# Attention and token/channel mixer on one core: strided loads ahead of the next x, the last group's u summed beforehand, a 128-row short chunk

## The chip, the cores and the metric

One core of a Trainium2 chip runs the kernel. The metric is device time of one execution in microseconds (us), lower is better, as the median of several timed runs. A profiled execution gives the trace that is read below; its span is the time from the first to the last instruction. The engines are TensorE (PE, with its weight loads PEld), VectorE (DVE), ScalarE (ACT), GpSimd (POOL) and SyncE (SP), which here issues every DMA.

## The reference

```
x  = concat over 8 heads of softmax(mask(q k^T / 8)) v      # 8 batches, 576 rows, 64 per head -> 512 columns
     heads 0-3: local mask (0 <= i-j < 32);  heads 4-7: strided mask (j <= i, i%32 == j%32)
h  = relu(x^T w_tok1) w_tok2                                # token mix: 576 -> 256 -> 576
u  = x + h^T
out = u + relu(u w_ch1) w_ch2                               # channel mix: 512 -> 1536 -> 512
```

All of it is float32. In the strided heads each of 32 residues is an 18 by 18 attention.

## The kernel before

Every matrix product is made of three products of rounded parts (high by high, high by low, low by high), accumulated in PSUM: `xh`/`xlo`, `uh`/`ul`, `gh`/`gl` and the weights `t1h`/`t1l` and so on are such pairs. ACT makes the high part, DVE (for some weights POOL) the low part by subtraction.

The 8 x 576 rows go through the channel mix in nine groups of 512 (`mlp(grp, ...)`). A group has twelve up projections (L524, 12 matmuls each) and twelve down projections (L538, 12 matmuls each, into four PSUM tiles `acc`). Up projection fc+2 is written ahead of down projection fc. After a group, each `acc` gets `uh` (L560, DVE) and `ul` (L562, POOL, in the last group DVE) added into one of two `ot` buffers and is sent out (L563).

Between these matmuls PE does the work of the coming batches. The local heads go over PE (L170, L197, L207, softmax on DVE and ACT). The strided heads of batches 0 and 1 go over PE as well; those of batches 2 to 7 are made by `strided` without PE: POOL multiplies (L342, 27 products into two `sprod` buffers), DVE reduces each product (L343), then a softmax (L346 to L352) and 27 more pairs (L359, L361). The results go to DRAM (`xs<-sb`, L363), and `load_x` brings a batch's `x` back in (L370, L372), in five row chunks. There is one `x` buffer. `tok1` (token mix 1, L384 xh on ACT, L387 xlo on DVE, L396 matmuls) takes the chunks in turn, two banks of PSUM held; `tok2` (token mix 2, L427 transposes of x and L433) makes `u`.

576 rows are four chunks of 128 and one of 64. The fifth chunk stands in x twice, in rows 0 to 63 and 64 to 127. Its two terms for each half of the outputs are `(t1h[:64], xlo[:64])`, a matmul over 64 rows, and `(t1l[:], xh)` over 128 rows, in which `t1l` holds the rounded weights above and their low part below.

Order: up to the end of group 0 the instructions follow a list of step names, `ORDER`, each name one step of a generator; `in_order` chains every instruction to the one before it on its engine. The names that matter here: `A`/`D` up and down projections of group 0, `V0` the first local unit of batch 2, `Y0` to `Y3` the last 64 rows of batch 0 through `tok2`, four column blocks, in the order Y3, Y0, Y2, Y1; `X1` the loads of batch 1's x, `B` its `tok1`, `C` its `tok2`, and `G` the call `strided` for batch 2. `G` alone is not chained; like all later work it is placed by a scheduler that works from a timeline of its own, with instructions of `strided` given a low priority. Also, `do_strided` holds its instructions back until the latest `x` load has been issued:

```
with tc.issue_after(state["loaded"].ins):
    strided(sp, b, 3000)
```

Once placed, each engine's order is fixed: an instruction that waits holds up everything behind it on its engine. SP is one such queue for all DMAs.

## Time and profile before

| | |
|---|---|
| timed runs | 888.44, 886.46, 879.77 us; median 886.46 |
| profiled execution | 882.51 us, of which the span is 880.5 us |
| mean granted TensorE clock | 0.982 |
| busy share of the span | PE 94%, DVE 55%, POOL 46%, ACT 24% |

The runs lie within 1% of each other. PE's busy time counts the matmuls as they overlap in the pipeline, so 94% does not say that 6% are left. The span has three parts: some 80 us at the start, in which weights are converted and batch 0 goes through attention and token mixes; the stretch to some 680 us, in which PE's projections go along with POOL's and DVE's strided heads; and a last stretch with PE alone.

### The profile page before, as it was taken

What the parts mean: (1) busy time and instruction counts of PE and PEld (TensorE: products, weight loads), DVE (VectorE), ACT (ScalarE), POOL (GpSimd) and SP (SyncE); (2) the same over time, 40 slices, a digit from 0 to 9 for tenths busy, and PEclk for the clock granted to TensorE, in tenths of its full rate; (3) what the DMA queues carried; (4) which work ended last, traced back from release to release, by engine and by line L of the source; (5) the groups of instructions that cost most, each with busy time, mean ns of one, the idle gap of its engine ahead of it and who ended that gap; (6) DMA issues with size and microseconds to landing.
All of it is one profiled execution on the core that took longest, in us unless ns stands there. A gap on an engine that the chain in (4) does not pass through costs nothing.

```text
span 880.5 us, 16250 instructions
## 1 busy us (share of the span) xinstructions
PE 826.7 (94%) x6820; PEld 659.7 (75%) x6820; DVE 487.8 (55%) x941; ACT 208.5 (24%) x378; POOL 404.0 (46%) x385
## 2 busy tenths in 40 slices
PE   4588999799978999999999999999999999999996
PEld 3366787578856787787887887778788877888885
DVE  4789873667567755775577567645774222112112
ACT  3676652221112212211212112112111121111110
POOL 0112300786577765795679477845885002002000
PEclk9979999999998999999999999999999999999998
DMA  7647754302542323023402421223112001001001
GB/s 256 198 157 251 240 191 123 130 1 92 132 160 63 102 54 123 28 80 88 157 28 79 142 97 40 74 64 115 35 53 77 11 1 48 1 1 41 8 1 48
DMA packets 57639, 78.99 MB, mean 90 GB/s; under 512 B 18144, under 2 KB 39776, under 8 KB 57568
## 3 DMA queue, kind: packets, MB, share of 16 engines
q1 hardware_dynamic: 57568, 77.97, 27.5%
q8 instruction: 53, 0.87, 0.4%
q14 instruction: 18, 0.15, 0.1%
HBM read 59.54 MB, written 18.28 MB: 88 GB/s over the span
## 4 chain that ended last, share of the span: by engine, by line
PE 65%; POOL 13%; DVE 9%; DMA 7%; issue 2%; SPq 2%; ACT 1%; DVEq 0%; POOLq 0%; ACTq 0%
PE h L524 25%; PE acc L538 23%; POOL sprod L342 9%; PE t L433 6%; POOL sprod L359 4%; PE t L396 4%; DMA sb<-in_ks 3%; PE t L427 3%; DVE ss L343 2%; DMA lk<-in_kT 1%; PE t L207 1%; DVE xlo L387 1%; PE t L170 1%; SPq L372 1%; DMA xs<-sb 1%
## 5 line engine op out<-in xcount | busy, mean ns | idle before, releaser
L342 POOL TENSOR_TENSOR sprod<-sb,sa 128x576 f32<-128x576 f32 (+6 forms) x162 | 175.1, 1110 | 133.8 <-DMA sb<-in_ks 114.8
L359 POOL TENSOR_TENSOR sprod<-sa,ss 128x448 f32<-128x448 f32 (+7 forms) x162 | 162.9, 1038 | 34.3 <-DVE ss L352 24.9
L524 PE MATMUL h<-ul,w1h 128*128 128x512 f32 x432 | 170.7, 395 | 0.0
L524 PE MATMUL h<-uh,w1l 128*128 128x512 f32 x432 | 169.5, 392 | 0.0
L538 PE MATMUL acc<-gh,w2l 128*128 128x512 f32 x432 | 169.3, 392 | 0.0
L524 PE MATMUL h<-uh,w1h 128*128 128x512 f32 x432 | 168.4, 396 | 0.9 <-DVE gl L530 0.9
L538 PE MATMUL acc<-gl,w2h 128*128 128x512 f32 x432 | 168.7, 390 | 0.0
L538 PE MATMUL acc<-gh,w2h 128*128 128x512 f32 x432 | 165.6, 394 | 0.2 <-ACT gh L528 0.2
L530 DVE SCALAR_TENSOR_TENSOR gl<-h,gh 128x512 fp32r<-128x512 f32 x108 | 74.0, 686 | 141.5 <-ACT gh L528 141.3
L528 ACT ACTIVATE gh<-h 128x512 fp32r<-128x512 f32 x108 | 64.4, 599 | 317.7 <-PE h L524 304.3
L343 DVE TENSOR_REDUCE ss<-sprod 128x9 f32<-128x576 f32 (+6 forms) x162 | 90.8, 570 | 55.4 <-POOL sprod L342 54.3
L361 DVE TENSOR_REDUCE sb<-sprod 128x64 f32<-128x64 f32 (+8 forms) x162 | 91.4, 571 | 36.9 <-POOL sprod L359 35.9
L562 POOL TENSOR_TENSOR ot<-ot,ul 128x512 f32<-128x512 f32 x32 | 41.2, 1295 | 136.5 <-DVE ot L560 136.4
L524 PEld LDWEIGHTS h<-uh,w1h 128*128 128x128 f32 x432 | 81.0, 188 | 18.4 <-DVE gl L530 1.4
L538 PEld LDWEIGHTS acc<-gh,w2h 128*128 128x128 f32 x432 | 81.2, 188 | 17.6 <-ACT gh L528 0.7
L524 PEld LDWEIGHTS h<-uh,w1l 128*128 128x128 f32 x432 | 81.6, 189 | 16.7
L524 PEld LDWEIGHTS h<-ul,w1h 128*128 128x128 f32 x432 | 81.4, 189 | 16.8
L538 PEld LDWEIGHTS acc<-gh,w2l 128*128 128x128 f32 x432 | 81.1, 188 | 17.1
L538 PEld LDWEIGHTS acc<-gl,w2h 128*128 128x128 f32 x432 | 81.1, 188 | 16.3
L387 DVE TENSOR_TENSOR xlo<-x,xh 128x512 fp32r<-128x512 f32 (+1 forms) x45 | 40.0, 905 | 33.8 <-ACT xh L384 33.7
L438 DVE TENSOR_TENSOR ul<-t,uh 128x512 fp32r<-128x512 f32 (+7 forms) x64 | 28.8, 454 | 42.6 <-ACT uh L436 42.4
L436 ACT CAST uh<-t 128x512 fp32r<-128x512 f32 (+7 forms) x64 | 25.5, 399 | 108.8 <-PE t L433 108.7
(97 smaller groups left out, 881.0 us busy)
## 6 DMA issues: line engine op xcount, KB each, us to landing
w_raw<-in_w SPq DMA_DIRECT2D x24, 512.0 KB
out_t<-ot SPq DMA_DIRECT2D x36, 256.0 KB
lv<-in_vw SPq DMA_DIRECT2D x8, 520.0 KB
x<-xs SPq DMA_DIRECT2D x8, 512.0 KB
lv<-in_vw SPq DMA_DIRECT2D x6, 650.0 KB
xl<-lx SPq DMA_DIRECT2D x14, 256.0 KB
x<-xl SPq DMA_DIRECT2D x7, 512.0 KB
sa<-in_qs SPq DMA_DIRECT2D x6, 576.0 KB
```

The lines of the kernel that those rows point to most:

```text
L342: nc.gpsimd.tensor_tensor(out=pr, in0=k_t[:, n0:n0 + n], in1=q_t[:, i:i + 1].to_broadcast([P, n, D]), op=ALU.mult)
L343: nc.vector.tensor_reduce(out=s_t[:, i, n0:n0 + n], in_=pr, axis=AX.X, op=ALU.add)
L359: nc.gpsimd.tensor_tensor(out=pr, in0=v_t[:, d0:d0 + nd, :n], in1=s_t[:, i:i + 1, :n].to_broadcast([P, nd, n]), op=ALU.mult)
L361: nc.vector.tensor_reduce(out=o_t[:, i, d0:d0 + nd], in_=pr, axis=AX.X, op=ALU.add)
L387: nc.vector.tensor_tensor(out=xlo, in0=x, in1=xh.bitcast(F32), op=ALU.subtract)
L396: nc.tensor.matmul(ph[m], l, r, start=(c == 0 and k == 0), stop=(short and k == 1), skip_group_check=True)
L433: nc.tensor.matmul(pu[:, :n], l[:, cs], r[:, m, t0:t1], start=False, stop=(m == 1 and k == 2), skip_group_check=True)
L524: nc.tensor.matmul(ph, l[:, cc, fs], r, start=(cc == 0 and k == 0), stop=(cc == NCC - 1 and k == 2))
L528: nc.scalar.activation(out=gh, in_=ph, func=AF.Relu)
L530: nc.vector.scalar_tensor_tensor(out=gl, in0=ph, scalar=0.0, in1=gh.bitcast(F32), op0=ALU.max, op1=ALU.subtract)
L538: nc.tensor.matmul(acc[cc], l[:, fc, cs], r, start=(fc == 0 and k == 0), stop=(fc == NFC - 1 and k == 2))
L562: add.tensor_tensor(out=o_t, in0=o_t, in1=ul.bitcast(F32), op=ALU.add)
```

## The change

Four edits. (1) `G` moves in ORDER from behind `D10 V0 V0` to behind `Y3`, ahead of `X1`; its first two instructions, the loads of q and k (`sa`, `sb`), are now chained in the order, and for batch 2 the hold behind the x load is dropped. (2) In the last group, `uh + ul` is summed into `whole`, a tile in the place of `x`, during the group, and the sum is added to `acc` in one instruction at the end; each column block keeps a buffer of its own. (3) The last group's last two down projections are written as one, column block by column block. (4) The lower half of `t1h`'s fifth chunk is set to zero on POOL, once, and the 64-row matmul of token mix 1 becomes one over 128 rows.

```diff
+            differ("t2").memset(t1h[64:, NSC - 1].bitcast(F32), 0.0)
...
-                    terms = ((t1h[:64, c, ms], xlo[:64]), (t1l[:, c, ms], xh))
+                    terms = ((t1h[:, c, ms], xlo), (t1l[:, c, ms], xh))
...
-    ORDER = """... O A11 V0 Y3 A11 A11 Y0 Y3 Y3 Y2 Y0 Y0 Y1 Y2 Y2 D9 Y1 X1 Y1 V0 D10 V0 V0 G D11 V0 B ..."""
+    ORDER = """... O A11 V0 Y3 G A11 A11 Y0 Y3 Y3 Y2 Y0 Y0 Y1 Y2 Y2 D9 Y1 X1 Y1 V0 D10 V0 V0 D11 V0 B ..."""
...
-            if n != "G":
-                for i in traced[begun:]:
+            got = traced[begun:] if n != "G" else traced[begun:begun + 2]
+            for i in got:
...
-        def down_proj(fc):
-            gh, gl = g.pop(fc)
+        def down_proj(*fcs):
+            gs = [g.pop(fc) for fc in fcs]
             for cc in range(NCC):
                 cs = slice(P * cc, P * cc + P)
-                for k, (l, r) in enumerate(((w2h, gh), (w2h, gl), (w2l, gh))):
-                    nc.tensor.matmul(acc[cc], l[:, fc, cs], r, start=(fc == 0 and k == 0), stop=(fc == NFC - 1 and k == 2))
+                for fc, (gh, gl) in zip(fcs, gs):
+                    for k, (l, r) in enumerate(((w2h, gh), (w2h, gl), (w2l, gh))):
+                        nc.tensor.matmul(acc[cc], l[:, fc, cs], r, start=(fc == 0 and k == 0), stop=(fc == NFC - 1 and k == 2))
...
-                run(down_proj(fc))
+                if grp < NG - 1 or fc < NFC - 2:
+                    run(down_proj(fc))
+                elif fc == NFC - 2:
+                    run(down_proj(fc, fc + 1))
...
+                if grp == NG - 1 and 4 <= fc < 4 + NCC:
+                    if fc == 4:
+                        whole = xp.tile([P, NSC, GT], F32, name="x", bufs=1)
+                    uh, ul = (u.bitcast(F32) for u in us[fc - 4])
+                    nc.vector.tensor_tensor(out=whole[:, fc - 4], in0=uh, in1=ul, op=ALU.add)
...
-            add = nc.vector if grp == NG - 1 else nc.gpsimd
-            add.tensor_tensor(out=o_t, in0=o_t, in1=ul.bitcast(F32), op=ALU.add)
+            if grp == NG - 1:
+                o_t = whole[:, cc]
+                nc.vector.tensor_tensor(out=o_t, in0=acc[cc], in1=o_t, op=ALU.add)
...
-        with tc.issue_after(state["loaded"].ins):
+        with tc.issue_after(state["loaded"].ins) if b > NSB else ExitStack():
```

What this does to the order on SP, around the loads of batch 1's x: first before, then now (line numbers of the changed kernel are one higher here). `sa` and `sb` are q and k of batch 2's strided heads, `lq`, `lk`, `lv` a local unit's operands, `xs<-lx` the last strided results of batch 1, `x` the loads of its x.

```order
L325 DMA xs_84<-lx 144x1x128 x4
L162 DMA lq<-in_qT 128x640
L163 DMA lk<-in_kT 128x672
L370 DMA x<-xl_76 128x4x256
L372 DMA x<-xl_76 64x256 x2
L370 DMA x<-xs_84 128x4x256
L372 DMA x<-xs_84 64x256 x2
L330 DMA sa<-in_qs 128x1152
L331 DMA sb<-in_ks 128x1152
L164 DMA lv<-in_vw 128x1300
```

```order
L326 DMA xs_84<-lx 144x1x128 x4
L163 DMA lq<-in_qT 128x640
L331 DMA sa<-in_qs 128x1152
L332 DMA sb<-in_ks 128x1152
L164 DMA lk<-in_kT 128x672
L371 DMA x<-xl_76 128x4x256
L373 DMA x<-xl_76 64x256 x2
L371 DMA x<-xs_84 128x4x256
L373 DMA x<-xs_84 64x256 x2
L165 DMA lv<-in_vw 128x1300
```

The two loads have moved ahead of six x loads, behind `lq`.

On DVE, around the last 64 rows of batch 0 (`gl` of up projection 11, the four `ul` of Y3, Y0, Y2, Y1) and batch 1's token mix 1 (`lz`, `lx` are the local unit's last steps, which give PSUM banks back; `ss` is the reduction of POOL's products), first before:

```order
L187 TENSOR_TENSOR ls<-ls,lm 128x640
L530 SCALAR_TENSOR_TENSOR gl<-h,gh 128x512
L438 TENSOR_TENSOR ul<-t,uh 128x64 x4
L215 TENSOR_SCALAR lz<-t 128x5 x2
L343 TENSOR_REDUCE ss<-sprod 128x1
L216 RECIPROCAL lz<-lz 128x10
L343 TENSOR_REDUCE ss<-sprod 128x2
L232 TENSOR_TENSOR lx<-t,lz 128x5x64 x2
L387 TENSOR_TENSOR xlo<-x,xh 128x512 x2
```

and now:

```order
L188 TENSOR_TENSOR ls<-ls,lm 128x640
L344 TENSOR_REDUCE ss<-sprod 128x1
L532 SCALAR_TENSOR_TENSOR gl<-h,gh 128x512
L344 TENSOR_REDUCE ss<-sprod 128x2
L439 TENSOR_TENSOR ul<-t,uh 128x64
L344 TENSOR_REDUCE ss<-sprod 128x3
L439 TENSOR_TENSOR ul<-t,uh 128x64
L344 TENSOR_REDUCE ss<-sprod 128x4
L439 TENSOR_TENSOR ul<-t,uh 128x64
L344 TENSOR_REDUCE ss<-sprod 128x5
L439 TENSOR_TENSOR ul<-t,uh 128x64
L344 TENSOR_REDUCE ss<-sprod 128x6
```

Reductions of POOL's products now stand ahead of `gl` and of each `ul`; six more follow, then `lz`, one reduction, `lx` and `xlo`.

On DVE, around batch 2's token mix 1 (the products are now those of batch 3's strided heads; `ot` is group 1's result), first before:

```order
L343 TENSOR_REDUCE ss<-sprod 128x1
L560 TENSOR_TENSOR ot<-acc_2546,uh 128x512
L215 TENSOR_SCALAR lz<-t 128x4 x2
L343 TENSOR_REDUCE ss<-sprod 128x9
L216 RECIPROCAL lz<-lz 128x8
L343 TENSOR_REDUCE ss<-sprod 128x2
L560 TENSOR_TENSOR ot<-acc_2547,uh 128x512
L232 TENSOR_TENSOR lx<-t,lz 128x4x64 x2
```

and now:

```order
L577 TENSOR_TENSOR ot<-acc_2547,uh 128x512
L344 TENSOR_REDUCE ss<-sprod 128x6
L216 TENSOR_SCALAR lz<-t 128x4 x2
L217 RECIPROCAL lz<-lz 128x8
L233 TENSOR_TENSOR lx<-t,lz 128x4x64 x2
L344 TENSOR_REDUCE ss<-sprod 128x9
L577 TENSOR_TENSOR ot<-acc_2548,uh 128x512
L344 TENSOR_REDUCE ss<-sprod 128x7
L388 TENSOR_TENSOR xlo<-x,xh 128x512 x2
```

The place of `lx` has moved from behind the 13th of the 27 products to behind the 21st.

## Rows read from the trace of the kernel before

**Rows 1.** Stage table: busy us and count of PE, PEld, DVE, ACT, POOL; PEclk, DMA share, GB/s

```profile
260.00:280.00 20.00, 15.07 (x103) 10.27 (x107) 14.01 (x23) 3.52 (x6) 14.78 (x15) 0.74 0.29 97
```

**Rows 2.** Timeline of PE, batch 2's token mix 1: start, us, instruction [idle before, releaser]

```profile
256.23 0.51 PE L538 MATMUL acc<-gh,w2l 128*128 128x512 f32 x1
262.50 0.77 PE L396 MATMUL t<-xh,t1h 128*128 128x512 f32 x1 [5.76 <-DVE lx L232]
...
270.45 0.50 PE L396 MATMUL t<-xlo,t1h 128*128 128x512 f32 x1 [1.88 <-DVE xlo L387]
...
275.74 0.50 PE L396 MATMUL t<-xh,t1l 128*128 128x512 f32 x1
```

**Rows 3.** Timeline of DVE, the same stretch

```profile
261.94 0.75 DVE L232 TENSOR_TENSOR lx<-t,lz 128x256 f32<-128x256 f32 x2
...
267.37 3.63 DVE L387 TENSOR_TENSOR xlo<-x,xh 128x512 fp32r<-128x512 f32 x2
...
272.33 0.69 DVE L387 TENSOR_TENSOR xlo<-x,xh 128x512 fp32r<-128x512 f32 x1 [1.01 <-ACT xh L384]
```

**Rows 4.** Timeline of SP: when the DMAs are issued

```profile
139.06 0.41 SPq L162 DMA_DIRECT2D lq<-in_qT  x1
...
150.89 0.43 SPq L331 DMA_DIRECT2D sb<-in_ks  x1
...
419.76 0.43 SPq L331 DMA_DIRECT2D sb<-in_ks  x1
```

**Rows 5.** Timeline of POOL: products of batches 2, 3 and 5

```profile
158.12 1.96 POOL L342 TENSOR_TENSOR sprod<-sb,sa 128x64 f32<-128x64 f32 x4 [28.85 <-DMA sb<-in_ks]
...
232.84 0.37 POOL L337 MEMSET ss<- 128x324 f32 x1
248.52 9.28 POOL L342 TENSOR_TENSOR sprod<-sb,sa 128x64 f32<-128x64 f32 x11 [15.31 <-DMA sb<-in_ks]
...
425.58 9.29 POOL L342 TENSOR_TENSOR sprod<-sb,sa 128x64 f32<-128x64 f32 x11 [17.61 <-DMA sb<-in_ks]
435.45 1.85 POOL L342 TENSOR_TENSOR sprod<-sb,sa 128x576 f32<-128x576 f32 x2 [0.58 <-DVE ss L343]
437.76 2.01 POOL L342 TENSOR_TENSOR sprod<-sb,sa 128x576 f32<-128x576 f32 x2 [0.45 <-DVE ss L343]
```

**Rows 6.** Timeline of PE around the last rows of batch 0 and batch 1's token mix 1

```profile
145.52 0.27 PE L427 MATMUL t<-ident,x 64*128 64x64 f32 x1
...
157.23 0.39 PE L538 MATMUL acc<-gh,w2l 128*128 128x512 f32 x1
159.71 0.47 PE L396 MATMUL t<-xh,t1h 128*128 128x512 f32 x1 [2.10 <-DVE lx L232]
```

**Rows 7.** Timeline of DVE, last rows of batch 0

```profile
144.88 0.22 DVE L438 TENSOR_TENSOR ul<-t,uh 128x64 fp32r<-128x64 f32 x1
```

**Rows 8.** Token mix 1 by line: duration ns min/median/max, start us, shapes

```profile
L396 PE MATMUL t<-xlo,t1h x90: 281/395/792, 37.0 to 711.1; 128*128 128x512 f32 x56, 128*128 128x256 f32 x16, 64*128 64x512 f32 x14, 64*128 64x256 f32 x4
```

**Rows 9.** Timeline of PE, short chunk of batch 3 between projections

```profile
355.04 0.39 PE L538 MATMUL acc<-gh,w2l 128*128 128x512 f32 x1
355.36 0.50 PE L396 MATMUL t<-xlo,t1h 64*128 64x512 f32 x1
...
356.97 0.39 PE L538 MATMUL acc<-gh,w2h 128*128 128x512 f32 x1
357.20 0.39 PE L538 MATMUL acc<-gl,w2h 128*128 128x512 f32 x1
```

**Rows 10.** The end: timelines of PE and DVE

```profile
872.18 0.39 PE L538 MATMUL acc<-gh,w2l 128*128 128x512 f32 x1
...
870.85 1.29 DVE L560 TENSOR_TENSOR ot<-acc,uh 128x512 f32<-128x512 f32 x2 [5.08 <-PE acc L538]
...
876.12 1.28 DVE L562 TENSOR_TENSOR ot<-ot,ul 128x512 f32<-128x512 f32 x2
```

**Rows 11.** The end: chain that ended last, start us, us

```profile
872.76 2.00 DMA out_t<-ot
```

More of the change, by code (lines that the diff above doesn't have):

```diff
@@ new lines, in attn_mixer_kernel @@
+    ORDER = """S0 L0 S1 u2 t0 u1 L1 S0 S0 L0 S0 L0 S0 S0 S0 L0 S0 L0 L0 S0 u2 S1 S0 t0 u2 L0 S0 S1 t1 L2 u2 t0 S1 S1 L0 u0 t0 S1 t0 u2 L1 L0 u1 S1 L1 S1 t1 u1 S1 L2 L1 S1 t2 u1 t1 u1 L1 S1 L1 L2 w1 t1 u0 t1 L1 X0 L3 L1 t2 u0 L1 Ta0 Ta1 L2 Ta0 w4 u0 L2 t2 Ta0 L2 u0 L2 w0 t2 Ta1 Tb0 t2 L2 Ta1 w1 Tb0 L2 L3 Tb0 L3 Tb1 Tb2 Tb1 w4 Tb2 Tb1 L3 w1 L3 Tb3 Tb2 L3 Tb3 w2 w1 L3 w4 Tb3 Tb4 Ta2 Tb4 w0 w3 Ta2 Tb4 L3 Ta2 L3 Tb5 w0 w4 Tb5 w9 w0 w4 Ta3 Ta4 Ta3 w2 Ta4 Ta3 w3 w2 Ta4 Ta5 w3 w5 w2 Ta5 w12 w3 w2 U0 w3 w9 w9 w5 U1 w7 w9 w5 U0 U2 w5 U0 U1 w5 w12 U1 U3 U2 w12 w7 U2 w12 w7 U3 U3 | w1 S3 w0 w9 w16 S3 w6 w12 w10 w7 w7 S3 w16 A0 w6 w16 S3 S3 A0 A1 w6 S3 w8 w16 w16 A0 w11 w6 S3 w6 A1 A2 S3 w10 w8 A1 w10 S3 A2 D0 M1 S3 w20 w10 A3 A2 S3 w10 w8 w11 w13 M1 D1 w8 w11 A3 w8 M1 w17 w11 w11 w20 A4 A3 M1 w20 w13 w14 w20 w13 M1 D2 A4 w20 M1 A4 w19 w17 w13 w17 M1 w13 D3 M0 M1 w21 w17 w14 w17 M1 w14 w19 A5 w19 w15 w14 M0 A5 w14 A6 w22 w19 M0 w19 w21 D4 w21 A6 M0 w15 A5 w23 w21 w15 M0 D5 M0 w21 w18 w15 A6 w22 w15 M0 A7 S2 M0 w23 w22 M0 w22 w23 A8 A7 w22 w23 A7 w18 w23 S2 A9 A8 S2 A8 S2 w18 S2 A10 S2 w18 w18 S2 E V0 D6 S2 S2 A10 D7 S2 A10 S2 V0 A9 D8 A9 V0 O A11 V0 Y3 G A11 A11 Y0 Y3 Y3 Y2 Y0 Y0 Y1 Y2 Y2 D9 Y1 X1 Y1 V0 D10 V0 V0 D11 V0 B V0 B0 B1 B0 B1 B0 B2 B1 B2 B3 B2 B3 B4 B3 B4 B4 B5 B5 C0 C0 C1 C0 C1 C2 C1 C2 C3 C2 C3 C3"""
@@ L474, in in_order @@
             next(steps[n], None)
-            if n != "G":
-                for i in traced[begun:]:
-                    if i.engine in last:
-                        tc.add_manual_dep(i, last[i.engine], mybir.DependencyInfo(mybir.DependencyClass.NoSync, mybir.DependencyReason.DATA), reason="order")
-                    last[i.engine] = i.name
+            got = traced[begun:] if n != "G" else traced[begun:begun + 2]
+            for i in got:
+                if i.engine in last:
+                    tc.add_manual_dep(i, last[i.engine], mybir.DependencyInfo(mybir.DependencyClass.NoSync, mybir.DependencyReason.DATA), reason="order")
+                last[i.engine] = i.name
     with tc.tile_pool(name="first", bufs=2) as first, \
@@ L558, in mlp @@
         for cc, (uh, ul) in enumerate(us):
-            o_t = up.tile([P, GT], F32, name="ot", bufs=2)
-            nc.vector.tensor_tensor(out=o_t, in0=acc[cc], in1=uh.bitcast(F32), op=ALU.add)
-            add = nc.vector if grp == NG - 1 else nc.gpsimd
-            add.tensor_tensor(out=o_t, in0=o_t, in1=ul.bitcast(F32), op=ALU.add)
+            if grp == NG - 1:
+                o_t = whole[:, cc]
+                nc.vector.tensor_tensor(out=o_t, in0=acc[cc], in1=o_t, op=ALU.add)
+            else:
+                o_t = up.tile([P, GT], F32, name="ot", bufs=2)
+                nc.vector.tensor_tensor(out=o_t, in0=acc[cc], in1=uh.bitcast(F32), op=ALU.add)
+                nc.gpsimd.tensor_tensor(out=o_t, in0=o_t, in1=ul.bitcast(F32), op=ALU.add)
             nc.sync.dma_start(out=outT[P * cc:P * cc + P, GT * grp:GT * grp + GT], in_=o_t)
```

1 line of the change is left out of this document (removed).

## The prediction

> **What bounds the kernel now.** I began with the stage table. Between the start and the end PE is busy almost without a break in most slices of 20 us; the worst is 260 to 280 us, with 15.07 us busy and a granted clock of 0.74 [rows 1], that is with parts at the lower of TensorE's two levels, 1.2 instead of 2.4 GHz. A matmul of 512 columns in a full stream takes a pitch of 0.23 us (356.97 to 357.20) [rows 9], and what counts is where PE leaves that pitch, not its busy share. The timeline of PE shows four such places: the start, batch 1's token mix 1, batch 2's token mix 1, and the end. Token mix 1 has 28 such matmuls, 6.4 us. For batch 2 PE is free of the projections at 256.5 and starts the last of the 28 at 275.74 [rows 2]: 19 us for 6.4.
>
> Why it waits there is read in DVE's queue. PE needs a PSUM bank that `lx` gives back; `lx` needs nothing but PE's own result, yet it starts at 261.94 [rows 3], because reductions of POOL's products stand ahead of it. POOL began this batch's products at 248.52 [rows 5]. POOL's chain of batches 2 and 3 is late as a whole: it begins at 158.12, after 28.85 us without work, waiting for `sb` [rows 5], whose load was issued at 150.89 [rows 4] behind batch 1's x loads, which themselves wait for PE to be done with the old x.
>
> **The change part by part.**
>
> *The loads ahead of x.* SP issues `lq` at 139.06 and is then free [rows 4]; now `sa` follows at about 139.5 and `sb` at about 140.1, some 10.8 us earlier than at 150.89. Before, POOL's first product stands 7.23 us behind the issue of `sb` for batch 2 and 5.82 us for batch 5 (419.76 to 425.58) [rows 4, 5]. With no x loads ahead of it I take 6.2, near the shorter one, and both ends as bounds: POOL starts at 146.3 (145.9 to 147.3), 11.8 us earlier (10.8 to 12.2). The Trainium skill (DMA: Bandwidth & Descriptors, section Anatomy of one DMA) has a fixed 2.0 us and then 436 KB per us; by an estimate from that, 1.5 MB issued from 139.06 land near 144.6; POOL would then start 1.5 us earlier still, and the sum would be 1.5 us larger.
>
> *What that does on DVE, batch 1.* The order now has a reduction ahead of `gl` and of each `ul`. The `ul` of Y3 started at 144.88 and ended at 145.1 [rows 7]; PE's transpose of Y2, which needs the bank that this `ul` frees, stood at 145.52 [rows 6]. Now DVE waits for POOL's first product. From POOL's start to that `ul`'s end I count a product of about 0.35 (the first four take 1.96 [rows 5]), two small reductions, `gl` and `ul`, 1.5 us in all: 147.8. PE therefore gets a new wait of 2.3 us (1.9 to 3.3) in the middle of batch 0's last rows, and the x loads of batch 1, which follow on PE's last transpose, move by as much. In return `lx` need no longer wait for POOL: in POOL's run of 11 products in 9.28 us [rows 5] the twelfth, the one ahead of `lx`, is there at about 157.2, while PE, moved by 2.3, comes at 159.8 instead of 157.5. The wait of 2.10 us before batch 1's token mix 1 [rows 6] goes. These two cancel to within a microsecond. On either side they don't set the end of this section, since the next stage hangs on POOL.
>
> *Batch 2's token mix 1.* POOL's products of batch 3 began 90.4 us after those of batch 2 (158.12 to 248.52) [rows 5]. In between lie 54 products, their reductions, three transfers and a softmax, ending with the memset at 232.84; nothing of that changes in number. So I move the start by the same 11.8 us to 236.7. The order now wants 21 products instead of 13 ahead of `lx`: 9.29 us for the first 11, then five pairs at a pitch of 2.31 us (435.45 to 437.76) [rows 5], 20.8 us, to 257.5; with the last reduction `lx` starts at about 258.4 instead of 261.94 [rows 3], 3.5 us earlier. The third chunk's `xlo` stood 5.4 us behind `lx` and the last matmul 8.4 us behind that (267.37, 275.74) [rows 2, 3]. If both distances stay, the stage ends 3.5 us earlier; this is the low bound. I expect them to shrink: PE's matmuls there ran in part at the lower clock after a wait of 5.76 us and another of 1.88 [rows 2], and with waits of 1 to 2 us less of that should be left; and the DVE order has one `ot` less and two reductions less between `lx` and `xlo`. At the full pitch all 28 matmuls right behind 256.5 would end 12.8 us earlier; that is the high bound. I take 7.5 us for everything up to the end of this stage, with the short chunks of batches 1 and 2 in it, near the middle and 4 us above the low end because the idle time is the part that a trace shows to be curable.
>
> Against this stands another row: two `xlo` took 3.63 us there and a single one 0.69 later on [rows 3]. POOL was multiplying during the former. The Trainium skill (SBUF — State Buffer, section SBUF: two separate sides) says that a DVE instruction with two SBUF inputs and a GpSimd one that reads SBUF lock each other out for a whole instruction. By that rule the change works against itself: POOL now runs its widest products while DVE makes batch 1's five `xlo`, and each could wait for one. The trace agrees in direction, though part of the 3.63 us is a wait for `xh`. By rows it is at most 1.1 us each; since batch 1's stage no longer sets the end, I add nothing to the sum and leave 2 us of the range to it.
>
> *The 128-row short chunk.* Between two projections of batch 3, four matmuls of the short chunk take from 355.04 to 356.97, 1.93 us over five pitches, where 5 x 0.23 = 1.13 would do [rows 9]. The two of them that are over 64 rows are the only ones of another shape, and the pitch is long on entering and on leaving each. There are 14 of them in the 512-column form, two a batch for batches 1 to 7 [rows 8]: 0.80 us a batch. Batches 1 and 2 are in the 7.5 us above; batches 3 to 7, whose token mix lies between projections on a busy PE, give 5 x 0.80 = 4.0 us (bounds 0, if the row count isn't the cause, and 4.0). The four of 256 columns in batch 0 I count at 0, since PE waits for a transfer of later strided heads soon after (0 to 0.8). The memset is one small POOL instruction at 39 us, ten microseconds before the first matmul that reads it, on an idle POOL: nothing.
>
> *The end.* The last matmul starts at 872.18 and its result is there at 872.57; the last DVE instruction ends at 877.40 [rows 10], because eight additions of 0.6 us run in two buffers and the second pair of blocks waits for a transfer of 2.00 us [rows 11]. Now one addition a block is left and each has its buffer; three blocks are finished while PE still works (the scheduler has spread the combined projection so that `acc` 0 to 2 end 8, 6 and 4 matmuls before the last), so the last addition ends 0.7 us behind PE instead of 4.8. That is 4.1 us; four transfers now leave close together, for which I take 0.3 off: 3.8 us (3.0 to 4.1). The four additions beforehand fall into a stretch in which DVE has little to do: nothing; without that cover they would cost 4 x 0.69.
>
> **Sum.** 7.5 + 4.0 + 3.8 = 15.3 us off the profiled execution's own 882.51 gives 867.2. The median of the timed runs lies 4 us above that execution, with runs on either side of it; I add 1 and predict **868 us**. Two measurements of this kernel can hardly be told apart within 1%.
>
> **Rivals.**
> (a) *The wait moves along.* The scheduler placed the reductions by its own timeline, which was too early by about 5 us at batch 2 (`lx` at 261.94 where PE came at 256.5). If it is so again, only the low bound comes, 3.5 + 4.0 + 3.8 = 11.3 with the short chunks of batches 1 and 2 swallowed, or, if `sa` and `sb` are held up on SP and the move does nothing, 9.4: 872 to 875. For it: 21 products ahead of `lx` instead of 13 use up most of the head start.
> (b) *All waits go*: 12.8 instead of 7.5 and perhaps 2 us in later batches: 861. Against it: a new wait at Y2.
> (c) *Rows are not why the short chunk is slow*: 4.0 + 1 less: 873. Against it: the pitch changes exactly at the 64-row matmuls.
> (d) *Slower.* With POOL ahead, reductions and their softmax stand ahead of `gl` in every batch's order, on DVE and ACT. A `gl` has two blocks of 12 matmuls, 5.4 us, less 1.3 for its own making: 4.1 us of slack. From a lateness above that PE stops in each of six batches; at 8 us it would be 3.9 x 6 = 23 us, and 868 + 23 = 891, slower than before. Against it: before, later batches show hardly a wait of PE.
>
> **How the numbers follow.** Chances: forecast 0.55 (861 to 871), (a) 0.18, (b) 0.13, (c) 0.07, (d) 0.07. The range of 8 in 10 takes in (b), (c) and most of (a): 858 to 878. Faster by over 1% (under 877.6) is all but (d) and a part of (a): 0.84; within 1%: 0.12; slower: 0.04.
>
> **What would show it.** In the profile after: POOL's first product near 146 instead of 158; a new wait of about 2 us of PE in batch 0's last rows; `lx` of batch 2's stage no longer followed by an idle PE of over 3 us, and a clock near 1 there; four matmuls of the short chunk at the plain pitch in batches 3 to 7; and at the end some 4 us from the last matmul to the end of the span instead of 8. I am wrong if POOL starts early and PE nevertheless stops for as long, at batch 2 or in later batches, with DVE's queue held by a reduction.

## The result, and the profile after

The changed kernel took 877.32 us (median of 11 runs, 872.78 to 879.99) against 882.44 us of the kernel before (11 runs). The ratio is 0.9929, with a 95% interval of 0.9909 to 0.9949: 6.3 us less by the ratio, 4.5 to 8.0 by its interval. That lies at the upper edge of the prediction's range (858 to 878), which was wide enough to take in rival (a), and well short of the 14 us that 868 meant. The profiled execution is the slowest of the 11, 879.99 us with a span of 877.6. Single executions of one kernel differ by several microseconds, mostly at the start, where PE waits for transfers: in the 14 traces of this document the first up projection starts between 70.2 and 74.2 us. So traces are compared by stage.

A ruler for that: the up-projection's matmuls, 144 to a group. Every version has the same 1296 of them in the same order, so the 97th, the 145th (the first of group 1) and the 289th (the first of group 2) can be found in each timeline of PE. "Stage 1" runs from the 97th to the 145th (batch 0's last rows and batch 1's token mixes lie in it), "stage 2" from there to the 289th (batch 2's lie in it), "rest" from there to the last matmul, "end" from there to the end of the span. Each is a difference of two starts.

| profiled execution | 97th | 145th | 289th | last matmul | span | stage 1 | stage 2 | rest | end |
|---|---|---|---|---|---|---|---|---|---|
| before | 119.19 | 174.65 | 279.01 | 872.18 | 880.5 | 55.5 | 104.4 | 593.2 | 8.3 |
| changed | 120.63 | 177.59 | 281.98 | 873.29 | 877.6 | 57.0 | 104.4 | 591.3 | 4.3 |

The end became 4.0 us shorter, stage 1 became 1.5 us longer, stage 2 did not move (the forecast had 7.5 us for everything up to its end), and the rest gained 1.9 us where 4.0 were forecast. Ahead of the 97th matmul 1.4 us were lost, where the first part of the change moves nothing. A second trace of the changed kernel (e13 below) has the same stages 1 and 2 within 0.1 us, but is 2.0 us shorter ahead of the 97th matmul and 1.3 us longer in the rest: differences of that size between two single traces show nothing.

The timeline of PE in the changed kernel, at the four places of which the prediction speaks, in the form of [rows 2, 6, 9, 10]:

```profile
148.66 0.27 PE L428 MATMUL t<-ident,x 64*128 64x64 f32 x1 [1.50 <-DVE ul L439]
...
244.96 1.21 PE L171 MATMUL t<-lk,lq 64*32 64x64 f32 x64 [1.43 <-issue]
...
261.12 0.40 PE L541 MATMUL acc<-gh,w2l 128*128 128x512 f32 x1
265.23 0.76 PE L397 MATMUL t<-xh,t1h 128*128 128x512 f32 x1 [3.71 <-DVE lx L233]
265.79 0.63 PE L397 MATMUL t<-xlo,t1h 128*128 128x512 f32 x1
266.22 0.63 PE L397 MATMUL t<-xh,t1l 128*128 128x512 f32 x1
...
272.77 0.50 PE L397 MATMUL t<-xlo,t1h 128*128 128x512 f32 x1 [2.32 <-DVE xlo L388]
...
276.94 0.40 PE L397 MATMUL t<-xh,t1l 128*128 128x512 f32 x1
...
356.35 0.39 PE L541 MATMUL acc<-gl,w2h 128*128 128x512 f32 x1
356.57 0.39 PE L397 MATMUL t<-xlo,t1h 128*128 128x512 f32 x1
...
357.48 0.39 PE L541 MATMUL acc<-gh,w2l 128*128 128x512 f32 x1
...
873.29 0.39 PE L541 MATMUL acc<-gh,w2l 128*128 128x512 f32 x1
```

First, the wait at Y2 is there (148.66, 1.50 us). Second, batch 2's stage takes as long as it did, but not for the same reasons: PE is free at 261.5, stands for 3.71 us, runs at a pitch of 0.43 us (265.79 to 266.22), stands again for 2.32 us, and starts the last of the 28 matmuls at 276.94; in [rows 2] this was 256.5 to 275.74. From the start of stage 2 the last of the 28 comes 1.8 us earlier than before (99.3 for 101.1 us), although PE is free of the projections 1.8 us later (83.9 for 82.1). The 1.8 us are lost again behind it: 5.0 us instead of 3.3 to the end of the stage, at a granted clock of 0.67 instead of 1.00. Third, the short chunk does run at the plain pitch: five pitches from 356.35 to 357.48 are 1.13 us, where [rows 9] had 1.93.

What DVE did at Y2, ahead of and at batch 2's token mix 1, and at the end:

```profile
147.47 0.22 DVE L344 TENSOR_REDUCE ss<-sprod 128x1 f32<-128x64 f32 x1 [5.19 <-POOL sprod L343]
...
148.39 0.22 DVE L439 TENSOR_TENSOR ul<-t,uh 128x64 fp32r<-128x64 f32 x1
...
244.44 0.74 DVE L233 TENSOR_TENSOR lx<-t,lz 128x256 f32<-128x256 f32 x2
...
263.71 0.54 DVE L344 TENSOR_REDUCE ss<-sprod 128x6 f32<-128x384 f32 x1
...
264.66 0.76 DVE L233 TENSOR_TENSOR lx<-t,lz 128x256 f32<-128x256 f32 x2
...
268.04 0.69 DVE L577 TENSOR_TENSOR ot<-acc,uh 128x512 f32<-128x512 f32 x1 [1.28 <-DMA out_t<-ot]
...
269.70 3.62 DVE L388 TENSOR_TENSOR xlo<-x,xh 128x512 fp32r<-128x512 f32 x2 [0.44 <-ACT xh L385]
...
871.90 2.50 DVE L574 TENSOR_TENSOR x<-acc,x 128x512 f32<-128x512 f32 x4 [5.02 <-PE acc L541]
```

`lx` starts at 264.66, later than in [rows 3] (261.94), right behind the 21st reduction (263.71). At the end four additions take 2.50 us and overlap PE's last matmuls. At 244.96 there is a wait that the prediction did not have: PE's first scores of a local unit start 0.1 us behind the first of two `lx` (the pair runs from 244.44), and that `lx` and its `lz` now stand behind the first reductions of batch 3. All seven traces with early loads have this wait, 1.3 to 2.4 us, each time 0.1 us behind an `lx`; none of the seven with late loads has it. The profile names no releaser, so that PE waits for the bank which `lx` gives back is read from these times. POOL shows where the head start went, and SP why:

```profile
147.12 1.28 POOL L343 TENSOR_TENSOR sprod<-sb,sa 128x64 f32<-128x64 f32 x3 [16.42 <-DMA sb<-in_ks]
...
222.94 0.37 POOL L338 MEMSET ss<- 128x324 f32 x1
241.16 4.91 POOL L343 TENSOR_TENSOR sprod<-sb,sa 128x64 f32<-128x64 f32 x7 [17.85 <-DMA sb<-in_ks]
```

```profile
223.22 0.38 SPq L371 DMA_DIRECT2D x<-xl  x1
...
224.90 1.07 SPq L364 DMA_DIRECT2D xs<-sb  x2
226.02 0.91 SPq L163 DMA_DIRECT2D lq<-in_qT  x1
226.97 1.36 SPq L164 DMA_DIRECT2D lk<-in_kT  x1
228.37 0.97 SPq L364 DMA_DIRECT2D xs<-sb  x2
232.68 0.38 SPq L371 DMA_DIRECT2D x<-xs  x1
...
234.94 0.43 SPq L332 DMA_DIRECT2D sb<-in_ks  x1
```

POOL's first product came 11.0 us earlier (147.12 for 158.12 [rows 5]), its memset behind batch 2's work 9.9 us earlier (222.94 for 232.84), its first product of batch 3 only 7.4 us earlier (241.16 for 248.52). On SP the four stores `xs<-sb` now stand behind and between other issues: the last pair is issued from 228.37 on, 5.4 us behind the memset; in the kernel before all four are issued within 3.2 us of it.

### The profile page after: what moved, and what is told of

The parts are those of the page before. It is cut to its first block, busy times and chain, and to the rows that moved or that the text cites. A ratio compares the mean times of both kernels' runs of the same rounds, so it can differ in the third digit from the quotient of the medians.

```text
span 877.6 us, 16239 instructions
## 1 busy us (share of the span) xinstructions
PE 824.1 (94%) x6820; PEld 661.7 (75%) x6820; DVE 488.9 (56%) x941; ACT 207.4 (24%) x378; POOL 403.8 (46%) x386
## 4 chain that ended last, share of the span: by engine, by line
PE 62%; POOL 13%; DVE 10%; DMA 7%; SPq 3%; issue 3%; ACT 1%; DVEq 0%; POOLq 0%; ACTq 0%
PE h L526 25%; PE acc L541 22%; POOL sprod L343 10%; PE t L434 6%; DMA sb<-in_ks 4%; PE t L428 3%; DVE ss L344 2%; POOL sprod L360 2%; PE t L397 2%; DVE xlo L388 2%; PE t L171 1%; DMA lk<-in_kT 1%; PE t L208 1%; SPq L373 1%; PE t L309 1%
## 5 line engine op out<-in xcount | busy, mean ns | idle before, releaser
L388 DVE TENSOR_TENSOR xlo<-x,xh 128x512 fp32r<-128x512 f32 (+1 forms) x45 | 42.1, 956 | 30.7 <-ACT xh L385 30.6
```

The costliest lines, as they stand in the source:

```text
L388: nc.vector.tensor_tensor(out=xlo, in0=x, in1=xh.bitcast(F32), op=ALU.subtract)
```

## The experiments

All were timed beside the kernel before, whose median was 882.44 to 885.37 us there; the ratio is to the runs of before on the same chip, and versions are compared by it. "L" says where the loads of batch 2's strided heads stand (early: as in the changed kernel), "R" whether the short chunk has 128 rows, "E" whether the end is the new one, "order" what was added to DVE's order. Stage columns are from each one's profiled execution.

| run | L | R | E | order | median, us | ratio, 95% interval | stage 1 | stage 2 | rest | end |
|---|---|---|---|---|---|---|---|---|---|---|
| before | late | no | no | | | 1 | 55.5 | 104.4 | 593.2 | 8.3 |
| changed | early | yes | yes | | 877.32 | 0.9929 (0.9909 to 0.9949) | 57.0 | 104.4 | 591.3 | 4.3 |
| e13, the same again | early | yes | yes | | 878.90 | 0.9924 (0.9896 to 0.9952) | 56.9 | 104.3 | 592.7 | 4.3 |
| e1 | late | yes | yes | | 879.11 | 0.9947 (0.9926 to 0.9967) | 56.0 | 102.3 | 594.9 | 4.3 |
| e2 | early | no | no | | 885.56 | 1.0010 (0.9980 to 1.0039) | 58.1 | 104.4 | 593.9 | 8.3 |
| e3 | late | yes | no | | 882.19 | 0.9988 (0.9964 to 1.0012) | 56.3 | 102.4 | 592.3 | 8.3 |
| e4 | late | no | yes | | 880.55 | 0.9968 (0.9946 to 0.9990) | 55.9 | 102.6 | 595.6 | 4.3 |
| e6 | early | yes | yes | lx first | 877.43 | 0.9905 (0.9875 to 0.9935) | 58.6 | 101.1 | 588.9 | 4.3 |
| e7 | early | yes | yes | ul first | 876.64 | 0.9886 (0.9853 to 0.9919) | 55.6 | 105.6 | 589.7 | 4.3 |
| e8 | early | yes | yes | ul, lx first | 876.53 | 0.9903 (0.9870 to 0.9936) | 54.3 | 101.8 | 593.4 | 4.3 |
| e9 | early | yes | yes | ul, lx, xlo first | 874.93 | 0.9896 (0.9866 to 0.9926) | 54.1 | 98.1 | 596.1 | 4.3 |
| e12 | late | yes | yes | lx, xlo first | 881.14 | 0.9965 (0.9942 to 0.9988) | 57.4 | 95.9 | 600.0 | 4.3 |
| e10, light | late | no | no | | 875.04 | 0.9905 (0.9883 to 0.9928) | 55.8 | 102.5 | 586.5 | 8.3 |
| e11, light | late | yes | no | | 870.32 | 0.9845 (0.9820 to 0.9871) | 55.8 | 102.1 | 582.1 | 8.3 |

**The three parts one by one (e1 to e4).** The parts separate cleanly: with the loads late, the instructions of every engine stand in the order of before except for the memset and the program's last group. e1 is the changed kernel with its first part undone:

```diff
-... A11 V0 Y3 G A11 A11 Y0 Y3 ... V0 D10 V0 V0 D11 ...
+... A11 V0 Y3 A11 A11 Y0 Y3 ... V0 D10 V0 V0 G D11 ...
...
-            got = traced[begun:] if n != "G" else traced[begun:begun + 2]
-            for i in got:
+            if n != "G":
+                for i in traced[begun:]:
...
-        with tc.issue_after(state["loaded"].ins) if b > NSB else ExitStack():
+        with tc.issue_after(state["loaded"].ins):
```

> The changed kernel with its first part undone: the loads of batch 2's strided heads stand where they stood before, behind batch 1's x, and the 128-row short chunk and the new end are kept. Theory: the gain that was measured (882.4 to 877.3 us) is that of the end (3.8 to 4.0 us) and of the short chunk (about 0.8 us a batch), and the loads' move gives nothing or costs a few us (a wait of 1.5 us at Y2 with 3.4 us of lower clock behind it, and the same wait as before at batch 2). Then this kernel is no slower than the changed one: 872 to 877 us, 6 to 10 us below the kernel before. Rival: the loads' move is worth several us and the other two parts less than forecast. Then this kernel lies above the changed one, at 878 to 881 us.

e2 is the kernel before with these lines the other way round.

> The first part alone on the kernel before: loads of batch 2's strided heads ahead of batch 1's x, with the old 64-row short chunk and the old end. Theory: no gain, 881 to 886 us (the ratio to before 0.998 to 1.005). Rival (the move gives what the measured gain is short of the other parts' forecast, or more): 875 to 879 us.

e3 is the kernel before with the 128 rows alone:

```diff
+            differ("t2").memset(t1h[64:, NSC - 1].bitcast(F32), 0.0)
...
-                    terms = ((t1h[:64, c, ms], xlo[:64]), (t1l[:, c, ms], xh))
+                    terms = ((t1h[:, c, ms], xlo), (t1l[:, c, ms], xh))
```

> The short chunk in 128 rows alone on the kernel before; the order of the instructions on each engine is that of before, with one memset more on POOL. Theory: 0.8 us less in each of batches 3 to 7 and something less in batches 0 to 2, 4 to 5.6 us in all: 877 to 878.5 us. Rival (the row count is not what makes the pitch long, or other waits take the gain): 881 to 883 us.

e4 is the kernel before with the change's edits to `mlp` alone.

> The new end alone on the kernel before: the last group's u added up beforehand, the last two blocks of the down projection taken together, one addition a block. Theory: 3.8 to 4.0 us less, 878 to 879 us, and some 4 us from the last matmul to the end of the span instead of 8. Rival (the end's gain is partly lost because the combined projection or the additions hold PE up): 880 to 882 us.

The loads' move alone gave nothing that can be told from zero (1.0010; between 1.8 us less and 3.4 us more). The end alone gave 2.8 us by its ratio, 0.9 to 4.8 by its interval; every trace with it shows 4.0 us less behind the last matmul. The 128 rows alone gave 1.1 us, between a loss of 1 and a gain of 3, and both together 4.7. My theory was wrong on the second of these: it had 4 to 5.6 us for the rows, and by the times the rival ("other waits take the gain") was right. And e1 did not come out below the changed kernel, but some 2 us above it, less than the two intervals can tell apart. The medians of e1 and e4 fall in the ranges of their rivals, which were drawn from the 882.44 us of before; on this chip before took 884.45, and the 3.8 us forecast for the end lie within the interval of e4.

The traces show where a gain can go. PE's waits in the stretch from 285 to 870 us, first in the kernel before, then in e3 (us in total, times, longest us):

```profile
PE t L170 <- DVE ul L438: 1.2, 1, 1.2
PE t L396 <- DVE xlo L387: 0.7, 1, 0.7
PE h L524 <- DVE gl L530: 0.6, 1, 0.6
```

```profile
PE t L397 <- DVE xlo L388: 3.0, 3, 1.3
PE h L525 <- DVE gl L531: 1.7, 2, 1.1
PE t L171 <- DVE ul L439: 1.5, 2, 1.2
```

These three sum to 2.5 us before and to 6.2 in e3. My reading: PE comes earlier to `gl`, `ul` and `xlo`, and DVE, whose queue holds reductions of POOL's products and additions that wait for an out transfer, is no earlier. One such place in e3, DVE's timeline:

```profile
382.17 0.69 DVE L561 TENSOR_TENSOR ot<-acc,uh 128x512 f32<-128x512 f32 x1 [0.81 <-DMA out_t<-ot]
...
383.76 0.68 DVE L531 SCALAR_TENSOR_TENSOR gl<-h,gh 128x512 fp32r<-128x512 f32 x1
```

and PE's:

```profile
384.50 0.49 PE L525 MATMUL h<-uh,w1h 128*128 128x512 f32 x1 [1.08 <-DVE gl L531]
```

PE does not wait at this place in the kernel before. But e4, with the order of before, also has waits of 6 us in the rest, and the two traces of the changed kernel have 4.9 and 6.9, so waits alone prove nothing; a test was needed.

**Is the short chunk's gain real, and DVE what takes it (e10, e11)?** Both kernels leave out most of POOL's products for batches 3 to 7, and with them DVE's reductions (3 of 18 rows are made), so that both engines have time there; e10 has the old short chunk, e11 the new one.

```diff
-        for i in range(NJ):
-            for n0 in range(0, i + 1, NJ // 2):
+        for i in range(3 if b > 2 else NJ):
+            for n0 in range(0, i + 1, NJ // 2):
...
-        for i in range(NJ):
+        if b > 2:
+            nc.gpsimd.memset(o_t, 0.0)
+        for i in range(3 if b > 2 else NJ):
             n = i + 1
```

> The kernel before with most of POOL's products and their reductions left out for batches 3 to 7 (3 of the 18 rows of the causal products are made in either half; scores and outputs of the other rows are not computed), so that DVE and POOL have idle time there. It is the base of the next run. Theory: PE waits for DVE in few places behind 285 us (in the kernel before these waits are 3.8 us), and batch 2's token mix 1 loses the wait behind reductions: 870 to 876 us. Rival: DVE's work there holds nothing up, and the time is 881 to 885 us.

> The run before (most of POOL's products of batches 3 to 7 left out) with the short chunk in 128 rows; the order of all engines is the same but for the memset. Theory: the short chunk saves PE 0.7 to 0.8 us in each of batches 3 to 7, and in the full kernel it is PE's waits for DVE behind reductions that take most of it back; where DVE has time, 3.5 to 5 us of difference to the run before are seen. Rival: the pitch of the short chunk is won back by nothing but is not worth more than the 1 to 2 us seen in the full kernel: 0.5 to 2 us of difference here too.

870.32 against 875.04 us, with intervals that don't touch: 4.7 us. The rest became 4.4 us shorter (586.5 to 582.1). PE's only wait of over 0.2 us behind 285 us was 1.6 us in e10, and is this in e11:

```profile
PE h L527 <- DVE gl L533: 1.1, 1, 1.1
```

Without these 0.5 us of difference, 3.9 us remain for five batches, 0.8 us each. The chunk itself shows it too: with 64 rows it takes 1.93 us in each of these batches, with 128 rows 1.13. So the forecast was right for PE, and the gain reaches the end of the program where DVE and POOL have time. Which of the two engines takes it in the full kernel is not separated by this pair, since both were relieved; what PE waits for there is DVE's results.

The same pair shows something else, at batch 2. Hardly a reduction of batch 3 is left ahead of `lx`, PE's wait for it is 0.81 us (e10) and 1.39 us (e11) instead of 5.3 to 5.8 in before, e1, e3 and e4, and yet stage 2 has 102.5 and 102.1 us, as in the last three. DVE and PE in e10:

```profile
265.05 0.69 DVE L562 TENSOR_TENSOR ot<-acc,uh 128x512 f32<-128x512 f32 x1 [3.54 <-DMA out_t<-ot]
270.32 0.69 DVE L562 TENSOR_TENSOR ot<-acc,uh 128x512 f32<-128x512 f32 x1 [4.58 <-DMA out_t<-ot]
...
271.66 0.80 PE L398 MATMUL t<-xlo,t1h 128*128 128x512 f32 x1 [6.59 <-DVE xlo L389]
```

Two `ot` that wait for out transfers now stand ahead of `xlo`, and PE waits 6.59 us for it (6.01 in e11). So taking POOL's products away from ahead of `lx` doesn't by itself shorten this stage.

**What stands ahead in DVE's order (e7, e6, e8).** e7 splits `strided`: its loads stay where the change put them, and batch 2's first nine reductions are put, one behind the other, behind the last `ul` of batch 0's rows (`H` is the second half of the step).

```diff
-... Y1 X1 Y1 V0 D10 ...
+... Y1 X1 Y1 H V0 D10 ...
         nc.sync.dma_start(out=k_t, in_=ks[b])
+        yield
...
+            if n == "H":
+                behind = last[mybir.EngineType.DVE]
+                for i in [i for i in got if i.engine == mybir.EngineType.DVE][:9]:
+                    tc.add_manual_dep(i, behind, ...)
+                    behind = i.name
+                got = []
```

> The changed kernel with the loads of batch 2's strided heads as early as there, but with the first nine reductions in DVE's given order behind the last ul of batch 0's last rows, so that no ul waits for a product of POOL. Theory: the 1.5 us that PE waits at Y2 and the 3.4 us that it then loses at the lower clock go, and 1 us at most of a wait comes back ahead of batch 1's token mix 1; PE is 3 to 5 us earlier at 175 than in the changed kernel, and about 2 to 4 us of it are left at the end: 873 to 875 us. Rival: batch 1's stage and batch 2's hang on POOL, which now starts its third product 3 us later, so that what is won at Y2 is waited for at batch 1's or batch 2's token mix: 876 to 879 us.

e6 orders batch 3's reductions from the fifteenth on behind the `lx` of batch 2's stage (14 ahead of it; the changed kernel has 21). For that the call for batch 3 is written two steps later (in e8 too; three in e9 and e12):

```diff
+                if b == 3 and nred >= 14:
+                    tc.add_manual_dep(red.ins, (state["lx"] if nred == 14 else before).ins.name, ...)
...
-        at(HS * (b - 2) + 14, do_strided, b)
+        at(HS * (b - 2) + (16 if b == 3 else 14), do_strided, b)
```

> The changed kernel with one thing more: in DVE's order batch 3's reductions from the fifteenth on stand behind the lx that token mix 1 of batch 2 waits for (14 ahead of it instead of 21), and in a row behind one another. Theory: PE's wait of 3.7 us at 265 and the lower clock behind it come from the reductions ahead of lx; lx now starts as soon as PE is done with the projections, and the matmuls of batch 2's token mix 2 begin 3 to 5 us earlier than in the changed kernel (278.3 there). Of it 2 to 4 us are left at the end: 873 to 875 us. Rival: the place is set by something else (xlo beside POOL, PSUM banks, the out transfers), and holding POOL back by its two product buffers costs later what it gives here: 877 us or more.

e8 has both, with 12 reductions ahead of `lx`.

> Both of these edits together (12 reductions of batch 3 ahead of lx). Theory: the loads' move is worth what was forecast once no instruction that PE waits for stands behind a product in DVE's queue: 5 to 8 us less than the changed kernel, 869 to 873 us. Rival: what PE wins in the first 300 us it waits for afterwards, at gl, ul and xlo that stand behind reductions in later batches, since POOL and DVE set the pace there: 874 to 877 us.

Each edit does at its place what the theory said. With the early loads stage 1 is 56.9 to 58.6 us (changed, e13, e2, e6), with late loads 55.5 to 56.3 (before, e1, e3, e4, e10, e11; 57.4 in e12), and with `ul` first 54.1 to 55.6 (e7 to e9): the reductions ahead of `ul` cost some 1 to 3 us there. `lx` first brings stage 2 from 104.4 to 101.1 and 101.8. But the three medians lie within 1 us of one another, and by the ratios 2 to 4 us below the changed kernel, not the 5 to 8 that I expected of both edits. All three medians lie in the ranges of their rivals. The rival of e8 had the gain given back in the rest; its trace shows 593.4 us there against 591.3 and 592.7 in the two traces of the changed kernel, too little to settle it.

One part of the theory fell: e7 has no wait at Y2, and yet the lower clock came. The windows of e7 and of e3, which has the old order (us, then busy time of PE, PEld, DVE, ACT and POOL, granted clock, DMA share, GB/s):

```profile
148.00:152.00 4.00, 4.00 (x18) 3.46 (x18) 1.27 (x6) 0.42 (x2) 1.16 (x3) 0.57 0.38 106
152.00:156.00 4.00, 4.00 (x15) 3.12 (x14) 2.10 (x5) 0.02 (x1) 4.00 (x5) 0.58 0.68 224
```

```profile
148.00:152.00 4.00, 4.00 (x17) 3.60 (x17) 0.68 (x3) 0.55 (x3) 0.00 (x0) 0.55 0.25 61
152.00:156.00 4.00, 4.00 (x14) 3.11 (x13) 0.00 (x0) 0.00 (x0) 0.00 (x0) 0.60 0.94 309
```

The kernel before had 1.00 in both windows, and the changed kernel 0.61 and 0.53. It is not the change alone that brings the clock down there: all seven traces with early loads have the lower clock near 150 us, but so have four of the seven with late loads, e10 among them (0.75 and 0.50), which has nothing of the change.

What is left at batch 2 in e8 is seen on DVE and PE:

```profile
263.62 0.69 DVE L589 TENSOR_TENSOR ot<-acc,uh 128x512 f32<-128x512 f32 x1 [3.38 <-DMA out_t<-ot]
...
264.89 3.16 DVE L394 TENSOR_TENSOR xlo<-x,xh 128x512 fp32r<-128x512 f32 x2
```

```profile
258.31 0.47 PE L403 MATMUL t<-xh,t1h 128*128 128x512 f32 x1 [0.43 <-DVE lx L233]
...
266.26 0.50 PE L403 MATMUL t<-xlo,t1h 128*128 128x512 f32 x1 [4.19 <-DVE xlo L394]
```

`lx` is on time, and now `xlo` stands behind an `ot` that waits for its buffer.

**All of PE's inputs first (e9).** This is e8 with one step more: reductions from the thirteenth on, and the third and fourth `ot`, go behind the last `xlo`:

```diff
-                    tc.add_manual_dep(red.ins, (state["lx"] if nred == 12 else before).ins.name, ...)
+                    tc.add_manual_dep(red.ins, (state["xlo"] if nred == 12 else before).ins.name, ...)
...
+                if grp == 1 and cc == 2:
+                    tc.add_manual_dep(ot.ins, state["xlo"].ins.name, ...)
...
```

> The two edits of the run before together, carried one step further at batch 2: batch 3's reductions from the thirteenth on, and the third and fourth addition of ot, stand behind the last xlo of batch 2's token mix 1 in DVE's order. Theory: the wait of 4.2 us that was left there came from xlo standing behind an ot that waits for its buffer's out transfer (3.4 us) and behind reductions; now all three xlo follow lx, PE runs the 28 matmuls with a wait of at most 1 us and little at the lower clock, and the first up-projection behind batch 2 starts 4 to 6 us earlier than in the run with both edits. At the end 2 to 4 us of it are left: 872 to 875 us. Rival: it is given back behind 300 us, since POOL is held for longer: 876 to 878 us.

PE, DVE and POOL in e9:

```profile
261.34 0.47 PE L403 MATMUL t<-xh,t1h 128*128 128x512 f32 x1 [0.43 <-DVE lx L233]
...
268.54 0.39 PE L403 MATMUL t<-xh,t1l 128*128 128x512 f32 x1
...
377.15 0.80 PE L538 MATMUL h<-uh,w1h 128*128 128x512 f32 x1 [2.60 <-DVE gl L544]
```

```profile
264.34 1.37 DVE L394 TENSOR_TENSOR xlo<-x,xh 128x512 fp32r<-128x512 f32 x2 [2.81 <-ACT xh L391]
```

```profile
258.68 2.52 POOL L595 TENSOR_TENSOR ot<-ot,ul 128x512 f32<-128x512 f32 x2 [4.13 <-DVE ot L589]
268.36 2.51 POOL L595 TENSOR_TENSOR ot<-ot,ul 128x512 f32<-128x512 f32 x2 [7.16 <-DVE ot L589]
```

The 28 matmuls now run from 261.34 to 268.54, 7.2 us, nearly the 6.4 of a full stream. Stage 2 is 98.1 us, 6.3 less than in the profile of before (which was the longest of those with late loads; e1, e3 and e4 had 102.3 to 102.6), and stage 1 is 1.4 us shorter: together 7.7 us, the size of the forecast's 7.5 (6.1 to 6.5 against e1, e3 and e4). The rest is 596.1 us, 3 us more than in the kernel before, but the traces with its order there (before, e1, e3, e4) spread from 592.3 to 595.6. What can be seen in it is a wait of 2.60 us for `gl` at 377, where the longest in e1 and e3 was 1.1, and a granted clock of 0.51 behind it (377 to 380). At 874.93 us it is the lowest median of a full kernel, 9.2 us (6.5 to 11.8) below the kernel before by its ratio; its interval still overlaps that of the changed kernel.

**Head start or order (e12, e13)?** e12 is e1 with the order of e9 at batch 2 (8 reductions ahead), without the loads' move.

> Loads of batch 2's strided heads where they stood before the change, 128-row short chunk and new end as in the changed kernel, and DVE's order at batch 2 as in the run with all xlo first: batch 3's reductions from the ninth on and the third and fourth ot behind the last xlo (8 products ahead of lx, since POOL starts batch 3 some 7 us later here). It tells whether the head start or the order is what counts. Theory: PE's loss at batch 2's token mix 1 comes from what stands ahead of lx and xlo in DVE's queue, so the order alone brings the stage as early as the loads' move with the order did (within 2 us, apart from the wait of 2 us ahead of batch 1's token mix 1 that stays), and the time is 874 to 877 us, below the changed kernel. Rival: without the head start POOL's reductions are missing later, PE waits for the second half of batch 3's x, and the time is 879 us or more.

> The changed kernel itself once more, beside the run above on one chip, to rank the versions and to see how far its waits and its start differ from one execution to the next. Theory: 876 to 879 us; the wait of 1.5 us at Y2 with the lower clock behind it, and the waits for lx and xlo at batch 2, are there again, each within 1 us.

e13 repeats stages 1 and 2 of the changed kernel within 0.1 us, although its single waits differ more than I expected (2.1 us for `lx` where there were 3.71): in these two traces the length of a stage is steadier than the waits in it.

On e12 neither side was right as put. The order alone shortens stage 2 most (95.9 us), 8.5 less than before: the gain at batch 2 needs no earlier loads, and without them PE is also spared the wait ahead of the local unit. But the rest takes it back: 600.0 us, 4.4 above the highest of the four just named. So the rival had the time right (879 us or more), though not the wait: PE waits for `ot` and `gl`, not for the second half of x. POOL's chain and the longest wait of PE in e12:

```profile
327.65 0.37 POOL L338 MEMSET ss<- 128x324 f32 x1
343.57 7.12 POOL L344 TENSOR_TENSOR sprod<-sb,sa 128x64 f32<-128x64 f32 x8 [15.55 <-DMA sb<-in_ks]
```

```profile
385.27 0.80 PE L531 MATMUL h<-uh,w1h 128*128 128x512 f32 x1 [2.57 <-DVE gl L537]
```

POOL ended batch 3 at 327.65 and began batch 4 at 343.57; in e1 it began at 339.08, in the changed kernel at 333.07, in e9 at 339.45. Ahead of the `gl` at 385 DVE has an `ot` that waits 1.35 us for an out transfer and softmax steps of batch 4 and of a local unit; the granted clock was 0.50 behind that wait (385 to 388). That holding the reductions of batch 3 is what puts them there, 100 us later, is likely but not shown. e9 is 6.1 us below e12 (0.9896 against 0.9965, intervals apart); besides the early loads it holds the reductions from the thirteenth on and not from the ninth, so the 6.1 us are not shown to be the loads' alone. Without the order the loads give nothing that can be told from zero (e2, and e1 against changed).

## Why the prediction was wrong, step by step

**The loads ahead of x: right up to POOL's start.** 147.12 stands for the forecast 146.3 (145.9 to 147.3); the load of `sb` itself was issued 1.3 us later than I assumed. The estimate from the Trainium skill (DMA: Bandwidth & Descriptors, Anatomy of one DMA), whose fit is for transfers issued from GpSimd while SP issues these, would have had POOL start 1.5 us earlier still. The trace doesn't bear it out: the first product stood 5.7 us behind the issue of `sb` (141.41 to 147.12), for which I had taken 6.2 from the nearest rows.

**Batch 1: the wait at Y2 came (1.50 us for 2.3), but "these two cancel to within a microsecond" held only in part.** The two waits did nearly cancel, 1.50 us new against 2.10 gone. But early loads without further order made stage 1 0.6 to 2.7 us longer than the late ones in e1, e3 and e4. For the changed kernel itself it is 0.7 us against e3, which has the lower clock near 150 us too, and 1.0 against e1 and e4, which kept the full one. The reason that I gave for adding nothing, that the next stage hangs on POOL anyway, held only as long as stage 2 was late.

**Batch 2's token mix 1: the step that failed.** It took 7.5 us off up to the end of this stage, on the ground that an earlier POOL makes `lx` earlier and that little else holds the stage; measured were 1.5 us more in stage 1 and nothing less in stage 2. "So I move the start by the same 11.8 us to 236.7": it moved by 7.4, since SP's stores of the result now stood behind issues for x and batch 2's units. I had named SP's queue in rival (a) and not put it into the sum. "21 products instead of 13 ahead of `lx`" was counted rightly, and from 241.16 they last until 264.2, so that `lx` comes 6.3 us later than forecast. Ahead of all this PE lost 1.4 us at the local unit (244.96), a term that the sum did not have. The waits that I expected to shrink (7.5 us taken from between 3.5 and 12.8) came back for `lx`, an `ot` and `xlo`: below the low bound, which should have been zero. And `lx` was not the only limit: e10 and e11, nearly without reductions ahead of it, have the same stage 2, since `xlo` stands behind `ot` additions that wait for out transfers. Rival (a), to which I gave 0.18, is what happened; its time of 872 to 875 us was still too low, because it counted on the whole of the chunk's 4.0. e9 and e12 show that the size was not fanciful: the gain is there once nothing that waits for POOL or for a transfer stands ahead of PE's inputs. But in e12 it comes from the order alone, without an earlier POOL.

**The short chunk: mechanism right, size on PE right, what reaches the end wrong.** 0.80 us a batch was forecast, and 0.8 measured where DVE has time (e10, e11); in the full kernel 1 to 2 us of the 4.0 arrive (1.1 in e3, 1.9 for e1 against e4; neither is clear of zero). The 1.13 that the prediction writes for 5 x 0.23, which is 1.15, is what five plain pitches measure. The words "on a busy PE" took an engine without waits for one that sets the pace. DVE is close behind it at several places (e3 has single waits of up to 1.3 us, two of them at the short chunk itself), and the sum of separate gains could not hold. Rival (c), the row count, is refuted: the pitch is plain in every trace with 128 rows.

**The end: right.** 3.8 us forecast, 4.0 in every trace.

**`xlo` beside POOL: nothing was added, and the row was misread.** Of the 3.63 us in [rows 3] the first `xlo` took 3.03 and the second 0.68, so a single one lost 2.3 us and not at most 1.1. Nor was part of it a wait for `xh`: the `xh` of the second one ended at 268.61, and this `xlo` started at 270.31.

**Rival (d)** did not come: the longest wait for `gl` in the changed kernel's rest is 0.6 us. In e9 and e12 a wait for `gl` of this kind shows, at one place in the program and 2.6 us long.

So of 15.3 us the end's 4 arrived, 1 to 2 of the chunk's 4.0, and none of batch 2's 7.5.

**What stays open.** The give-back in the rest is shown as a sum and at its places, but which of DVE's instructions would have to move there was not tried, nor more buffers for `ot` or for the products. Whether e7 or e9 beats the changed kernel is likely (four versions with the edited order lie at 0.9886 to 0.9905, two measurements of the changed kernel at 0.9924 and 0.9929) but not settled for any single one.

## What to carry to other kernels

Before moving a producer earlier, list what the scheduler will put ahead of the waiting engine's inputs as a result, and count a gain only up to the next instruction that stands behind the producer in an in-order queue; the low bound of such a move is zero or below. A gain on the busiest engine is worth its size only if the engines that feed it have slack at each of their own deadlines: leave work out on the feeder, as e10 and e11 do, and see whether the gain appears. Leaving out the work that one is said to wait for also shows what stands next in line: e10 and e11 had the `ot` additions there. Two parts of a change can need one another: the early loads alone (e2) and the order alone (e12 against e1) measured as no gain, and together (e9) they gave the lowest median.

## What the hardware showed that I had not expected

The granted clock fell near 150 us with PE busy 4.00 of 4.00 us and no wait ahead (e7: 0.57 and 0.58; e3: 0.55 and 0.60), among the four blocks of matmuls of 64 columns of batch 0's last rows; in the kernel before, which has the order of e3 there, it stayed at 1.00. At the lower level, 1.2 GHz, a matmul of 512 columns has a pitch of 0.43 us, as from 265.79 to 266.22 above. So one trace's full clock at such a place is no promise for the next.

Two `xlo` of 128 x 512 took 3.62 and 3.16 us while POOL multiplied (changed, e8) and 1.37 us while POOL stood still (e9). The Trainium skill (SBUF — State Buffer, SBUF: two separate sides) says that a VectorE instruction with two SBUF inputs and a GpSimd instruction that reads SBUF shut each other out for a whole instruction; these rows agree: in the changed kernel the first `xlo` took 3.02 us, from 269.70 to 272.72, while two POOL instructions ran back to back from 269.65 to 272.17, and ended 0.55 us behind them; the second took 0.68.
